# Causal attention and a hardswish feed-forward: the products of weights and v of two pairs of heads in one stretch of TensorE

## The chip, the cores and the metric

The kernel runs on one core of one Trainium2 chip. The metric is the device time of one launch in microseconds (us); lower is better. A core has five engines with a queue each, which meet only at semaphores: PE (TensorE, matrix products, with PEld for its weight loads), DVE (VectorE), ACT (ScalarE), POOL (GpSimd) and SP (SyncE, which issues this kernel's transfers).

## The reference

q, k and v are 4 batches x 12 heads x 448 positions x 64, in float32.

```python
scores = scale * np.matmul(q, k.transpose(0, 1, 3, 2))
scores = np.where(np.triu(np.ones((seq, seq), dtype=bool), k=1), -1000000000.0, scores)
scores = scores - np.max(scores, axis=-1, keepdims=True)
attn = np.exp(scores)
attn = attn / (np.sum(attn, axis=-1, keepdims=True) + 1e-09)
x = np.matmul(attn, v)        # then heads side by side: 1792 rows of 768
h = x @ w_in                  # 768 -> 2048
g = h * np.clip(h + 3.0, 0.0, 6.0) / 6.0
out = g @ w_out               # 2048 -> 768
```

## The kernel before

**Tiling.** The 448 positions of a batch are four tiles of 112. Heads are worked on in pairs, six pairs to a batch. The first 112 positions of all four batches are done first, for each pair (`first_pair`). The other 336 positions of one pair of one batch are the work of `pair(n)`, n = 6 x batch + p, which is called 24 times: scores for three tiles (lines 450 and 451, in batch 0 line 453), masking and row minimum on DVE (L476), exponentials with row sums on ACT (L483), the inverse (L492, L493), the scaling of the weights on POOL (L505), nine transposes on PE in three blocks (L516), a copy of each block out of PSUM into a tile `pt` (through `move`, L238 or L241), and the product with v (`times_v`, L535). That product has eight matmuls: four tiles of positions times two heads. One head's result goes to partitions 0 to 63 of the PSUM bank `av`, the other's to 64 to 127. Its operands are float32, and the trace shows each of them as two matmuls, 16 for a pair.

**Splitting.** `x_split` then takes the bank and makes two float32r tiles of it, `xh` (rounded) and `xl` (the rest). Its steps are a rounding copy on ACT or DVE, for batches 0 and 1 also a plain copy to `r` on ACT, and a subtraction on POOL or DVE. The feed-forward part runs in five groups (`group(g)`): group 0 has 448 columns (first tiles of all batches), groups 1 to 4 the 336 remaining ones of one batch each. Every product is done three times (lines 598 to 600: high x high, high x low, low x high). A chunk of weights is loaded, in group 0 decoded on DVE (L571 to L576, in a PSUM bank `s`), and split into `wh` (ACT) and `wl` (DVE or POOL). A group is 576 matmuls; I call them G below. Group g takes x of batch g-1, and its first G comes 576 G after that of the group before. While a group runs, the attention of a later batch is slipped in between its chunks.

**What sets the order.** All work is recorded as operations with a key (a due time in steps), a duration, the engines that may take it, and the buffers it needs. `Flow.run` plays this forward with its own durations and gives each engine a fixed list: an engine takes the ready operation with the lowest key for which all buffers are free. Buffers are counted by kind: `pt0`, `pt1`, `pt2` 4 each (a pair needs two of each), `vr` 3, `xh` and `xl` 8, `r` 4, and the PSUM banks `s` 6 and `mo` 2. A `pair` has key t = 16 n - 16 (in batch 0: 13 n + 4), and its `times_v` key t + 15.9. `times_v` is recorded as `tiled`, for which the planner adds 0.1 us when PE goes from an untiled operation to a tiled one or back.

Of the kernel before, what the change touches and what calls it, by code (L numbers as in the profile page):

```python
# [43 lines left out]
R = S - C  # L44
# [146 lines left out]
def tile_causal_attention_hardswish_moe(ctx: ExitStack, tc: tile.TileContext, q, k, v, w_in, w_out, out):  # L191
# [13 lines left out]
    def buf(tag, shape, dt=F32):  # L205
        return Buf(tag, shape, dt)

    def bank(tag):
        return Buf(tag, [128, 512], F32)

    def ap(b):
        if b.tile is None:
            b.tile = pools[b.tag].tile(b.shape, b.dt, tag=b.tag, name=b.tag)
        return b.tile

    def f(x):
        return x.bitcast(F32)


    def one(key, ways, dur, emit, r, w):  # L220

        ways = {e: x if isinstance(x, tuple) else (x, 0) for e, x in ways.items()}
        flow.op(key, ways, [(dur, emit, w)], r)

    def pe(key, parts, r, tiled=False):
        flow.op(key, {"PE": (1, 0)}, [(d, lambda e, g=g: g(), w) for d, g, w in parts], r, tiled)
# [7 lines left out]
    def move(key, n, o, i, r, w, ways=None, scale=None):  # L234

        def emit(e):
            if e == "A":
                nc.scalar.copy(o(), i()) if scale is None else nc.scalar.mul(o(), i(), scale)  # L238
            elif e == "D":
                if scale is None:  # L240
                    nc.vector.tensor_copy(o(), i())  # L241
                else:
                    nc.vector.tensor_scalar(o(), i(), scale, None, ALU.mult)
            else:
                nc.gpsimd.tensor_scalar(o(), i(), 1.0, 1.0, ALU.mult, ALU.mult)  # L245
        one(key, ways or {"A": 1}, (n + 200) / 1200, emit, r, w)

    def minus(key, n, o, a, b, r, w, ways):
        def emit(e):
            (nc.gpsimd if e == "P" else nc.vector).tensor_tensor(o(), a(), b(), ALU.subtract)  # L250
        one(key, ways, elem(n), emit, r, w)
# [25 lines left out]
    def x_split(key, g, p, av, n):  # L277
        xh, xl = buf("xh", [128, S], F32R), buf("xl", [128, S], F32R)
        x_t[g, p] = xh, xl
        move(key, n, lambda: ap(xh)[:, :n], lambda: ap(av)[:, :n], [(av, 0)], [(xh, 0)], {"A": 1, "D": (1, .5)})  # L280
        y = av
        if g < 2:
            y = buf("r", [128, S])
            move(key, n, lambda: ap(y)[:, :n], lambda: ap(av)[:, :n], [(av, 0)], [(y, 0)], {"A": 1})
        minus(
            key + .01, n, lambda: ap(xl)[:, :n], lambda: ap(y)[:, :n], lambda: f(ap(xh)[:, :n]),
            [(y, 0), (xh, 0)], [(xl, 0)], {"P": 2.4, "D": (1, 1.0)} if g < 2 else {"D": 1},
        )
# [117 lines left out]


    TILES = (3, 2, 1)

    def pair(n):  # L410
        b, p = divmod(n, NPAIR)
        t = T_REST + 16 * n if b else T_EARLY + 13 * n
        vr = buf("vr", [C, NC_, 2, D])
# [12 lines left out]
        if b:  # L426
            for e in range(2):
                x, y, z = qk[e], op[e], kl[e]
# [12 lines left out]
        st = buf("prow", [C, 2, 8])  # L441
        ps = {(e, i): bank("s") for i in TILES for e in range(2)}
        pr = {(e, i): buf(f"pr{i}", [C, C * (i + 1)]) for i in TILES for e in range(2)}

# [49 lines left out]

        sums = [(st, e, 4 + i) for e in range(2) for i in TILES]
        one(t + 4, {"D": 1}, .45, inverse, [], sums)
        pt = {}
        for e in range(2):
            for i in reversed(TILES):
                def scaled(g, e=e, i=i):  # L500
                    x, r = ap(pr[e, i]), ap(st)[:, e, 4 + i:5 + i]
                    if g == "A":
                        nc.scalar.mul(x, x, r)
                    else:
                        nc.gpsimd.tensor_scalar(x, x, r, 1.0, ALU.mult, ALU.mult)  # L505
# [23 lines left out]
        av = bank("s")  # L529
# [7 lines left out]
                        start=(j == 0), stop=(j == NC_ - 1),  # L537
                    )

        pe(t + 15.9, [(1.9, times_v, [(av, 0)])], [(vr, 0)] + [(x[0], 0) for x in pt.values()], True)  # L540
        x_split(t + 16, b + 1, p, av, R)


    def cols(i):
# [119 lines left out]
    for g in range(B + 1):  # L664
        if g:
            for p in range(NPAIR):
                pair(NPAIR * (g - 1) + p)
        group(g)
# [41 lines left out]
```

## Time and profile before

| | |
|---|---|
| median of 3 runs | 661.43 us (659.28 to 661.99) |
| profiled execution | 661.54 us, of it span 659.8 us |
| PE busy | 643.9 us, 98% |
| DVE, ACT, POOL busy | 465.8, 367.3, 301.2 us |
| mean TensorE clock granted | 0.992 |

The span is the time between the first and the last instruction; the profiled execution took 1.74 us more than it. A row of the timeline gives start, length, engine, line, operation and tiles. The lengths of PE's matmuls overlap, so what one costs is read from start to start. In the change's file the lines from 409 on are numbered one higher, and those behind `times_v` six higher (L535 is L536 there, L598 to L600 are L604 to L606).

### The profile page before, as it was taken

What the parts mean: (1) busy time and instruction counts of PE and PEld (TensorE: products, weight loads), DVE (VectorE), ACT (ScalarE), POOL (GpSimd) and SP (SyncE); (2) the same over time, 40 slices, a digit from 0 to 9 for tenths busy, and PEclk for the clock granted to TensorE, in tenths of its full rate; (3) what the DMA queues carried; (4) which work ended last, traced back from release to release, by engine and by line L of the source; (5) the groups of instructions that cost most, each with busy time, mean ns of one, the idle gap of its engine ahead of it and who ended that gap; (6) DMA issues with size and microseconds to landing.
All of it is one profiled execution on the core that took longest, in us unless ns stands there. A gap on an engine that the chain in (4) does not pass through costs nothing.

```text
span 659.8 us, 12245 instructions
## 1 busy us (share of the span) xinstructions
PE 643.9 (98%) x4236; PEld 587.3 (89%) x4236; DVE 465.8 (71%) x939; ACT 367.3 (56%) x870; POOL 301.2 (46%) x333
## 2 busy tenths in 40 slices
PE   7689999999999999999999999999999999999998
PEld 5569887878889999999999999999999999999997
DVE  4889898977687798854588795567798743566432
ACT  3665656654546666555576664656666554444342
POOL 1667667546572686423375563433676410011100
PEclk9979999999999999999999999999999999999999
DMA  9989876888788543556744547555553334643452
GB/s 232 259 267 298 265 242 192 260 282 295 206 265 246 158 144 107 159 171 182 217 152 135 154 127 206 157 168 186 161 168 87 112 113 132 209 139 110 139 164 65
DMA packets 66878, 120.89 MB, mean 183 GB/s; under 512 B 16896, under 2 KB 33408, under 8 KB 66816
## 3 DMA queue, kind: packets, MB, share of 16 engines
q1 hardware_dynamic: 66816, 120.11, 60.7%
q8 instruction: 33, 0.54, 0.3%
q14 instruction: 29, 0.24, 0.1%
HBM read 101.99 MB, written 18.09 MB: 182 GB/s over the span
## 4 chain that ended last, share of the span: by engine, by line
PE 92%; DVE 3%; DMA 1%; SPq 1%; ACT 1%; POOL 1%; issue 1%; DVEq 0%; ACTq 0%; POOLq 0%
PE mo L598 24%; PE mo L600 23%; PE mo L599 23%; PE s L535 6%; PE s L516 6%; PE s L450 3%; PE s L451 2%; PE s L453 2%; DMA gh<-in_k_dram 1%; SPq L229 1%; PE s L399 1%; DVE s L571 1%; DVE s L573 1%; DVE op L576 0%; PE s L329 0%
## 5 line engine op out<-in xcount | busy, mean ns | idle before, releaser
L250 DVE TENSOR_TENSOR wl<-wd,wh 128x512 fp32r<-128x512 f32 (+1 forms) x159 | 142.8, 898 | 99.8 <-ACT wh L238 99.5
L238 ACT CAST wh<-wd 128x512 fp32r<-128x512 f32 (+1 forms) x160 | 112.9, 706 | 120.0 <-PE mo L599 85.9
L598 PE MATMUL mo<-xh,wh 128*128 128x336 f32 (+1 forms) x480 | 160.8, 335 | 0.1
L598 PE MATMUL mo<-gh,wh 128*128 128x336 f32 (+1 forms) x480 | 159.2, 332 | 0.0
L600 PE MATMUL mo<-xh,wl 128*128 128x336 f32 (+1 forms) x480 | 157.2, 327 | 0.0
L600 PE MATMUL mo<-gh,wl 128*128 128x336 f32 (+1 forms) x480 | 156.9, 327 | 0.3 <-POOL wl L250 0.3
L599 PE MATMUL mo<-gl,wh 128*128 128x336 f32 (+1 forms) x480 | 156.4, 326 | 0.0
L599 PE MATMUL mo<-xl,wh 128*128 128x336 f32 (+1 forms) x480 | 156.2, 325 | 0.0
L505 POOL TENSOR_SCALAR pr<-pr,prow 112x224 f32<-112x224 f32 x144 | 109.0, 773 | 39.5 <-DVE prow L493 39.3
L476 DVE CUSTOM_DVE_ANT_0 s<-s,mask 112x448 f32<-112x448 f32 (+1 forms) x144 | 70.6, 527 | 39.7 <-PE s L451 33.1
L245 POOL TENSOR_SCALAR gh<-r 128x336 fp32r<-128x336 f32 x51 | 33.3, 654 | 138.2 <-DVE r L627 128.6
L598 PEld LDWEIGHTS mo<-xh,wh 128*128 128x128 f32 x480 | 91.0, 190 | 5.8 <-issue 1.7
L598 PEld LDWEIGHTS mo<-gh,wh 128*128 128x128 f32 x480 | 90.3, 188 | 2.8 <-issue 0.8
L599 PEld LDWEIGHTS mo<-xl,wh 128*128 128x128 f32 x480 | 91.4, 190 | 1.1
L600 PEld LDWEIGHTS mo<-gh,wl 128*128 128x128 f32 x480 | 90.2, 188 | 2.2 <-POOL wl L250 0.6
L600 PEld LDWEIGHTS mo<-xh,wl 128*128 128x128 f32 x480 | 90.6, 189 | 1.3
L599 PEld LDWEIGHTS mo<-gl,wh 128*128 128x128 f32 x480 | 90.3, 188 | 1.3
L483 ACT ACTIVATE pr<-s,prow 112x448 f32<-112x448 f32 (+1 forms) x144 | 76.9, 542 | 25.7 <-DVE prow L476 25.7
L250 POOL TENSOR_TENSOR wl<-op,wh 128x512 fp32r<-128x512 f32 (+1 forms) x35 | 53.3, 1522 | 44.1 <-ACT wh L238 34.3
L238 ACT COPY pt<-s 112x336 f32<-112x336 f32 x139 | 53.3, 446 | 26.0 <-PE s L516 25.9
L621 ACT ACTIVATE r<-mo,three 128x336 f32<-128x336 f32 (+1 forms) x80 | 44.7, 558 | 26.4 <-PE mo L600 20.9
L245 POOL TENSOR_SCALAR op<-qk 128x784 fp32r<-128x784 f32 x31 | 30.4, 985 | 57.3 <-PE s L451 54.0
(70 smaller groups left out, 853.6 us busy)
## 6 DMA issues: line engine op xcount, KB each, us to landing
wd<-kept_w SPq DMA_DIRECT2D x64, 384.0 KB, 3.3
wd<-kept_w SPq DMA_DIRECT2D x96, 256.0 KB, 2.7
wd<-in_w_in_dram SPq DMA_DIRECT2D x16, 768.0 KB, 5.7
wd<-in_w_out_dram SPq DMA_DIRECT2D x24, 512.0 KB, 5.2
qk<-in_k_dram SPq DMA_DIRECT2D x84, 112.0 KB, 2.7
qk<-in_q_dram SPq DMA_DIRECT2D x84, 84.0 KB, 2.6
kept_w<-op SPq DMA_DIRECT2D x16, 384.0 KB, 5.7
kept_w<-op SPq DMA_DIRECT2D x24, 256.0 KB, 5.4
```

The lines of the kernel that those rows point to most:

```text
L238: nc.scalar.copy(o(), i()) if scale is None else nc.scalar.mul(o(), i(), scale)
L245: nc.gpsimd.tensor_scalar(o(), i(), 1.0, 1.0, ALU.mult, ALU.mult)
L250: (nc.gpsimd if e == "P" else nc.vector).tensor_tensor(o(), a(), b(), ALU.subtract)
L476: lambda _, e=e, i=i, w=w, dst=dst: nc.vector.tensor_tensor_reduce(dst(), dst(), mask[:, S - w:], -0.125, 3.0e38, ALU.add, ALU.min, ap(st) ...
L483: lambda _, e=e, i=i, dst=dst: nc.scalar.activation(ap(pr[e, i]), dst(), ACTF.Exp, bias=ap(st)[:, e, i:i + 1], scale=-1.0, accum_out=ap(st ...
L505: nc.gpsimd.tensor_scalar(x, x, r, 1.0, ALU.mult, ALU.mult)
L516: nc.tensor.transpose(ap(tp)[:C, C * o:C * o + C], ap(pr[e, i])[:, C * j:C * j + C], ident)
L535: nc.tensor.matmul(ap(av)[64 * e:64 * e + 64, R - w:R], ap(vr)[:, j, e, :], ap(ph)[:, o:o + w], start=(j == 0), stop=(j == NC_ - 1),)
L598: nc.tensor.matmul(ps, ap(wh)[:, a], xh, start=start, stop=False)
L599: nc.tensor.matmul(ps, ap(wh)[:, a], xl, start=False, stop=False)
L600: nc.tensor.matmul(ps, ap(wl)[:, a], xh, start=False, stop=stop)
L621: lambda _, r=r, acc=acc: nc.scalar.activation(ap(r)[:, :n], ap(acc)[:, :n], ACTF.Relu, bias=three, scale=1.0),
```

## The change

The function `pair` no longer records its `times_v` and `x_split` at once. It puts them into a list `left`; every second pair (p odd) records one operation with two parts, the products of the pair before and its own, with the key of the second, and then both splits with that key.

```diff
     TILES = (3, 2, 1)
+    left = []
...
-        pe(t + 15.9, [(1.9, times_v, [(av, 0)])], [(vr, 0)] + [(x[0], 0) for x in pt.values()], True)
-        x_split(t + 16, b + 1, p, av, R)
+
+        left.append((p, av, times_v, [(vr, 0)] + [(x[0], 0) for x in pt.values()]))
+        if p % 2:
+            pe(t + 15.9, [(1.9, go, [(a, 0)]) for _, a, go, _ in left], [x for a in left for x in a[3]], True)
+            for u, a, _, _ in left:
+                x_split(t + 16, b + 1, u, a, R)
+            left.clear()
```

An operation needs all its buffers at its start: two banks `s`, and all twelve `pt`-tiles (four of each kind, two of each for either pair) stay taken until then.

On PE, in batch 1, this stood for its sixth pair before (s_3872 is the bank `av`, vr_3102 that pair's v):

```order
L599 MATMUL mo_3859<-gl_2624,wh_3788 128x336
L600 MATMUL mo_3859<-gh_2608,wl_3793 128x336
L535 MATMUL s_3872<-pt0_3804,vr_3102 64x336
L535 MATMUL s_3872<-pt0_3841,vr_3102 64x336
L535 MATMUL s_3872<-pt1_3818,vr_3102 64x336
L535 MATMUL s_3872<-pt1_3855,vr_3102 64x336
L535 MATMUL s_3872<-pt2_3821,vr_3102 64x224
L535 MATMUL s_3872<-pt2_3857,vr_3102 64x224
L535 MATMUL s_3872<-pt2_3821,vr_3102 64x112
L535 MATMUL s_3872<-pt2_3857,vr_3102 64x112
L450 MATMUL s_3886<-op_3694 112x448
L451 MATMUL s_3886<-kl_3711,op_3694 112x448
```

After the same G of the program the change has a stretch of sixteen. This is its seam, from the last two products of one pair (bank s_3857) on:

```order
L536 MATMUL s_3857<-pt2_3553,vr_2786 64x112
L536 MATMUL s_3857<-pt2_3589,vr_2786 64x112
L536 MATMUL s_3869<-pt0_3789,vr_3346 64x336
L536 MATMUL s_3869<-pt0_3826,vr_3346 64x336
L536 MATMUL s_3869<-pt1_3803,vr_3346 64x336
L536 MATMUL s_3869<-pt1_3840,vr_3346 64x336
L536 MATMUL s_3869<-pt2_3806,vr_3346 64x224
L536 MATMUL s_3869<-pt2_3842,vr_3346 64x224
L536 MATMUL s_3869<-pt2_3806,vr_3346 64x112
L536 MATMUL s_3869<-pt2_3842,vr_3346 64x112
L451 MATMUL s_3884<-op_3678 112x448
L452 MATMUL s_3884<-kl_3696,op_3678 112x448
```

One pair's products follow the other's with nothing between them. The place 96 G earlier, where the pair before had its own stretch, now goes from a G to a score product.

Over the whole of PE's list (from group 0's first G on) such stretches stand at 24 places before and at 12 now. Of transposes it has 52 runs before and 59 now, of scores (L450, L451, L453) 52 both times. The new runs come mostly in group 0. There the first pair of batch 1 had its nine transposes in one run:

```order
L600 MATMUL mo_2336<-gh_694,wl_2324 128x448
L516 MATMUL s_2365<-ident_121,pr1_2237 112x112
L516 MATMUL s_2365<-ident_121,pr2_2221 112x112
L516 MATMUL s_2365<-ident_121,pr3_2201 112x112
L516 MATMUL s_2370<-ident_121,pr1_2237 112x112
L516 MATMUL s_2370<-ident_121,pr2_2221 112x112
L516 MATMUL s_2370<-ident_121,pr3_2201 112x112
L516 MATMUL s_2376<-ident_121,pr2_2221 112x112
L516 MATMUL s_2376<-ident_121,pr3_2201 112x112 x2
L598 MATMUL mo_2336<-gh_694,wh_2357 128x448
```

Now they come block by block, with six G after each:

```order
L606 MATMUL mo_2253<-gh_694,wl_2301 128x448
L517 MATMUL s_2334<-ident_121,pr1_2146 112x112
L517 MATMUL s_2334<-ident_121,pr2_2131 112x112
L517 MATMUL s_2334<-ident_121,pr3_2092 112x112
L604 MATMUL mo_2253<-gh_694,wh_2287 128x448
L605 MATMUL mo_2253<-gl_706,wh_2287 128x448
L606 MATMUL mo_2253<-gh_694,wl_2301 128x448
L604 MATMUL mo_2253<-gh_694,wh_2287 128x448
L605 MATMUL mo_2253<-gl_706,wh_2287 128x448
L606 MATMUL mo_2253<-gh_694,wl_2301 128x448
L517 MATMUL s_2353<-ident_121,pr1_2146 112x112
```

On ACT, behind the last products of batch 0, the split of one pair stood between two castings of weights before:

```order
L238 CAST wh<-op 128x512
L238 CAST xh<-s 128x336
L238 COPY r<-s 128x336
L238 CAST wh<-op 128x512 x2
L483 ACTIVATE pr_2289,prow<-s,prow 112x224
```

Now two pairs are split there at a time; one of the two castings to `xh` is on DVE's list:

```order
L238 CAST wh<-op 128x512 x2
L484 ACTIVATE pr_2209,prow<-s,prow 112x224
L238 COPY r<-s 128x336
L238 CAST xh<-s 128x336
L238 COPY r<-s 128x336
L238 CAST wh<-op 128x512
```

## Rows read from the trace of the kernel before

**Rows 1.** The page: the chain that ended last, share of the span by engine.
```profile
PE 92%; DVE 3%; DMA 1%; SPq 1%; ACT 1%; POOL 1%; issue 1%; DVEq 0%; ACTq 0%; POOLq 0%
```

**Rows 2.** Windows: stretch, its length, busy us of each engine, clock, DMA.
```profile
62.70:162.00 99.30, 98.88 (x561) 81.37 (x561) 86.59 (x180) 56.60 (x134) 63.87 (x65) 1.00 0.81 255
162.00:206.00 44.00, 43.75 (x254) 36.90 (x255) 34.05 (x69) 23.11 (x57) 24.21 (x27) 1.00 0.78 241
206.00:552.70 346.70, 346.70 (x2413) 325.71 (x2411) 247.51 (x507) 211.30 (x508) 171.41 (x191) 1.00 0.52 154
```

**Rows 3.** Timeline of PE at the last pair: start us, length us, engine, line, operation.
```profile
550.60 0.32 PE L600 MATMUL mo<-gh,wl 128*128 128x336 f32 x1
550.85 1.92 PE L535 MATMUL s<-pt,vr 112*64 112x336 f32 x16
552.70 0.42 PE L598 MATMUL mo<-gh,wh 128*128 128x336 f32 x1
552.96 0.32 PE L599 MATMUL mo<-gl,wh 128*128 128x336 f32 x1
553.11 0.32 PE L600 MATMUL mo<-gh,wl 128*128 128x336 f32 x1
```

**Rows 4.** Timeline inside that stretch, by narrow windows: steps two, five and six.
```profile
551.18 0.73 PE L535 MATMUL s<-pt,vr 112*64 112x336 f32 x4
...
552.03 0.55 PE L535 MATMUL s<-pt,vr 112*64 112x224 f32 x4
...
552.22 0.46 PE L535 MATMUL s<-pt,vr 112*64 112x224 f32 x4
```

**Rows 5.** Timeline of PE: a stretch with scores behind it; scores alone.
```profile
206.19 0.32 PE L600 MATMUL mo<-xh,wl 128*128 128x336 f32 x1
...
207.94 0.32 PE L599 MATMUL mo<-xl,wh 128*128 128x336 f32 x1
...
285.88 0.32 PE L600 MATMUL mo<-gh,wl 128*128 128x336 f32 x1
...
289.66 0.32 PE L599 MATMUL mo<-gl,wh 128*128 128x336 f32 x1
```

**Rows 6.** Timeline of PE: scores of batch 0 alone, and with a stretch behind.
```profile
98.80 0.37 PE L600 MATMUL mo<-xh,wl 128*128 128x448 f32 x1
...
99.97 0.37 PE L599 MATMUL mo<-xl,wh 128*128 128x448 f32 x1
...
142.28 0.37 PE L600 MATMUL mo<-gh,wl 128*128 128x448 f32 x1
...
145.30 0.36 PE L599 MATMUL mo<-gl,wh 128*128 128x448 f32 x1
```

**Rows 7.** Timeline of PE around nine transposes, and around three.
```profile
89.25 0.36 PE L600 MATMUL mo<-xh,wl 128*128 128x448 f32 x1
...
90.54 0.36 PE L599 MATMUL mo<-xl,wh 128*128 128x448 f32 x1
90.74 0.36 PE L600 MATMUL mo<-xh,wl 128*128 128x448 f32 x1
...
94.25 0.36 PE L600 MATMUL mo<-xh,wl 128*128 128x448 f32 x1
...
94.96 0.36 PE L599 MATMUL mo<-xl,wh 128*128 128x448 f32 x1
```

**Rows 8.** The line of `times_v`: weight loads, ns least/median/most, first and last start.
```profile
L535 PEld LDWEIGHTS s<-pt,vr x384: 132/137/137, 75.5 to 552.4; 112*64 112x64 f32 x192
```

**Rows 9.** Timeline of PE at 184 us, with the idle time before a matmul.
```profile
184.18 0.37 PE L599 MATMUL mo<-gl,wh 128*128 128x448 f32 x1
184.80 0.47 PE L600 MATMUL mo<-gh,wl 128*128 128x448 f32 x1 [0.25 <-POOL wl L250]
```

**Rows 10.** Timeline of ACT in a split at 184 us.
```profile
183.99 0.44 ACT L238 CAST xh<-s 128x336 fp32r<-128x336 f32 x1 [0.60 <-PE s L535]
```

**Rows 11.** Timeline of PE: group 4's first product with x.
```profile
567.53 0.31 PE L598 MATMUL mo<-xh,wh 128*128 128x336 f32 x1
```

## The prediction

> **What bounds the kernel now.** I read the chain of waits first: PE holds 92% of it, and no other engine more than 3% [rows 1]. Then the busy times by stretch: from 62.7 us, where the first stage ends, to 552.7 us, where the last product with v ends, PE is busy for 98.88 of 99.30, 43.75 of 44.00 and all of 346.70 us [rows 2]. It is without work for 0.7 us in 490. DVE, the next, is at 87% in the first of these stretches and at 71% in the last. So in the part that the change touches a microsecond less on PE is one less in the span, and one that another engine gains gives nothing. What counts is what PE pays that is no column of a product. The clock is at its full level in all three stretches (granted 1.00, so 2.4 GHz), and PE doesn't rest in them, before or after; I take no term for it.
>
> **What one stretch of products with v costs.** Lengths overlap, so I read starts. Between G of 336 columns a step is 0.15 us (552.96 to 553.11). At the last pair [rows 3] the last G before starts at 550.60 and the second G behind at 552.96: 2.36 us, where two steps would be 0.31. The visit costs 2.05 us. Its own work is eight steps, one for each matmul of the program. The 336-column ones are 0.283 us apart (551.18 to 552.03 is three of them), a 224-column one 0.19 [rows 4]; 112 columns I put at half of that, 0.095. That makes 4 x 0.283 + 2 x 0.19 + 2 x 0.095 = 1.70 us. The remaining 0.35 us is the way in and out: the first product starts 0.25 after the last G instead of 0.15, the first step inside takes 0.33 (550.85 to 551.18) instead of 0.28, the last product needs 0.19 (two steps of 0.095 would end at 552.60, and G starts at 552.70), and the first G behind takes 0.26.
>
> With score products behind it, the visit from 285.88 to 289.66 is 3.78 us, and the same scores alone, 206.19 to 207.94, are 1.75 [rows 5]. The difference is 2.03: 1.70 of work and 0.33. With batch 0's scores ahead of it (themselves a product on half of the rows) it is 3.02 against 1.17 us [rows 6], a difference of 1.85, so only 0.15: leaving those scores costs much the same, and is saved.
>
> In PE's list before, eight of the 24 stretches stand between G, thirteen have scores of batches 1 to 3 on one or both sides, and three stand behind scores of batch 0. That is 8 x 0.35 + 13 x 0.33 + 3 x 0.15 = 7.5 us of ways in and out.
>
> **The change part by part.**
>
> Merging. PE's list now has 12 stretches of double length: three between G, eight beside scores, one behind scores of batch 0. 3 x 0.35 + 8 x 0.33 + 0.15 = 3.8 us, 3.7 less than before. The products themselves stay, 384 matmuls in the trace. That a seam between two pairs costs nothing is not in this trace, since no two pairs stand side by side. Its nearest row is a step inside a stretch, where other weights and other columns come in and the step is still 0.283 [rows 4]: no cost. The far bound is that a seam costs what a way in does, 0.10 + 0.05 us, for 12 seams 1.8 us. I take nothing, as the inner step is the same matter: same shape, same halves of the array.
>
> Transposes. Their runs go from 52 to 59, mostly in group 0, where single blocks of three now stand between G. Nine together, 89.25 to 90.54, are 1.29 us less two steps of 0.20, so 0.89; three, 94.25 to 94.96, are 0.71 less 0.40, so 0.31 [rows 7]. Three times three is 0.93, so two more visits cost 0.04. Seven cost 7 x 0.02 = 0.15 us. Score runs are as many as before; some now meet a G where they met a product with v. A visit of eight scores alone costs 1.75 - 0.31 = 1.44 us [rows 5], and its steps (four of about 0.20, four of 0.155) 1.43, so this is under 0.02 for each of some ten places. I put 0.1 to it, and 0.05 to a run of batch 0's scores that had transposes directly behind it and now has a G.
>
> Splits. Two banks come to be split at once. On ACT a casting to `xh` takes 0.44 us [rows 10], the copy to `r` as much, so a merged stretch brings up to 0.9 us more in one go to ACT in batches 0 and 1. That lies beside PE as long as `wh` and `wl` are ready ahead. Where that cover is gone PE waits for the part that sticks out; the trace has one such place, 184.80 us, where a G waits 0.25 us for `wl` from POOL [rows 9]. In groups 1 to 3 PE is never without work. I take no stall more than before, and between -0.3 (the one there goes) and 3 us for the range.
>
> Waiting for the second pair. The first pair of a couple has its products up to a pair's period later. Its x is wanted only in the next group. The tightest is the last couple, which ends where it ends now, at 552.70, and group 4 wants x at 567.53 [rows 11]: 14.8 us for splits of some 2 us. What is held longer are the `pt`-tiles, one `vr`, and `av` not at all, since both banks are taken only at the start. Transposes of the next pair must then wait for free tiles and banks, which in the list has PE do G in between; nothing is queued behind them. Weight and q, k loads on SP's queue keep their distance of chunks, though `vr` loads come later in it; they have a pair's period to arrive.
>
> **Sum.** -3.7 + 0.15 + 0.1 + 0.05 = -3.4 us. The profiled execution took 661.54 us (span 659.8 and 1.74 around it), 0.1 over the median of the three runs shown. 661.5 - 3.4 = 658.1, from the median 658.0. I say 658.1 us, 0.5% less than before.
>
> The Trainium skill speaks for a price of the seams. In "TensorE: Matmul & The Clock Gate", section "Measured speedup vs the span model" with "The mechanism" before it, a weight load runs beside matmuls in flight only when its row group is another. All products with v use the same 112 rows. By that rule each seam would show a load, 0.137 us in this trace [rows 8], 12 x 0.137 = 1.6 us, and the sum would be -1.8. The trace doesn't bear it out inside a stretch: the step of 0.283 has room for no load of its own, though each step has two matmuls with a load each.
>
> **The rivals.**
>
> *A seam costs a way in.* The first product of the second pair has waits of its own (for its v and for ACT's copies), and the 0.15 us of a way in could come from such waits and not from the change of halves. Against it: a run of transposes begins with a wait for POOL's scaling too, and yet a run more costs 0.02 us [rows 7]. Then 1.8 us of the gain go: 659.9 us, within 0.5%.
>
> *The splits stick out.* Group 0 has the thin cover: all of PE's 0.7 us without work lie in its two stretches [rows 2], and one piece of it was a wait for `wl` [rows 9]. If ACT's 0.9 us more came through in full at the three couples of batch 0, 2.7 us would go: 660.8 us. For it speaks that DVE is at 87% there, against it that ACT is at 57% (56.60 of 99.30). The Trainium skill, in "TensorEngine Tiling (Array Packing)", section "PSUM Bottleneck", says that tiling speeds up the products and not the emptying of PSUM, which may then be the limit; by that the price would be this rival's, and no row here has PE wait for a bank yet.
>
> *Slower: banks in the second half of group 0.* Decoding a chunk needs a bank `s`, and between 162 and 206 us six banks serve decoding, the scores and transposes of batch 1's first pairs, and now two results at once. The transposes that come block by block show that tiles or banks are short there. If decoding comes late, `wl` does, and a G waits as at 184.18, where a step of 0.20 took 0.62, 0.42 lost [rows 9]. If all 24 chunks of that half lost as much, 10 us would go: 668.2 us. It decides from 16 chunks on (16 x 0.42 = 6.7 us, the gain and 0.5%). Against it: before, one chunk did.
>
> **How the numbers follow.** A measurement of this kernel can tell about 0.5% from no change, 3.3 us: faster means under 658.1, slower over 664.7. The forecast lies on the first bound. Forecast (the full gain, stalls under 1 us, 657.2 to 659.0): 0.68, of which 0.37 falls under the bound, about half, as it should with the sum on it. Seam: 0.09. Splits sticking out: 0.15. Slower: 0.05. A gain over 4 us, by a stall that goes: 0.03. So faster 0.37 + 0.03 = 0.40, same 0.31 + 0.09 + 0.15 = 0.55, slower 0.05. The range is 656.9 to 660.6: below, the forecast's end and some of the runs' own spread; above, the seam's 659.9 and nearly all of the splits' 660.8.
>
> **What would show it.** In the profile after: 12 stretches of 32 matmuls; between the 16th and 17th start of one a step of 0.09 to 0.10 us, not 0.19 or more; a visit between G of 3.75 us (2 x 1.70 + 0.35) beside the 2.05 of now; PE without idle time from 62.7 us on, and the end of the last stretch at about 549 us. Wrong would be: longer seams, idle time of PE in front of L606 put down to `wl`, or before L517 to POOL or to a copy, above all between 160 and 206 us.

## The result, and the profile after

The change made the kernel slower: 666.44 us median of six runs (665.96 to 668.86) against 660.94 (659.28 to 661.99), a ratio of 1.0092 with a 95% interval of 1.0071 to 1.0113. I had forecast 658.1 us and given "slower" one chance in twenty. The profiled execution, 668.86 us with a span of 667.1, is the longest of the six. 1.6 us of what sets it apart lie ahead of the 79th G, where PE's list is still before's (PE waits 3.3 us behind the 36th; e7 and e8, with before's list, have such a wait there too), so below I compare stretches behind that.

The chain of waits first, where PE had 92% [rows 1]:

```profile
PE 78%; DVE 7%; DMA 5%; POOL 4%; issue 3%; SPq 1%; ACT 1%; DVEq 0%; POOLq 0%; ACTq 0%
```

Then the busy times by stretch (length, busy us of PE, PEld, DVE, ACT, POOL, clock, DMA share, GB/s), the last one up to the end of the last product with v:

```profile
62.70:162.00 99.30, 98.24 (x556) 81.15 (x557) 86.55 (x177) 57.87 (x137) 60.55 (x62) 1.00 0.81 250
162.00:206.00 44.00, 43.54 (x252) 37.12 (x249) 34.29 (x67) 21.81 (x55) 27.33 (x30) 1.00 0.74 231
206.00:559.69 353.69, 349.20 (x2428) 327.39 (x2426) 251.02 (x514) 210.16 (x507) 174.35 (x193) 1.00 0.53 155
```

PE was without work for 0.7 us in these three before [rows 2] and is for 6.0 now, 4.5 of it behind 206 us, where it never waited. The waits of PE behind 62 us (who for whom, us in total, times, longest):

```profile
PE mo L604 <- DVE r L633: 2.1, 3, 1.7
PE s L517 <- POOL pr L506: 1.4, 3, 0.5
PE s L451 <- ACT wh L238: 1.0, 2, 0.5
PE s L517 <- DVE op L582: 0.7, 1, 0.7
PE mo L606 <- POOL wl L250: 0.4, 1, 0.4
PE s L517 <- ACT pt L238: 0.2, 1, 0.2
```

Six kinds of wait, 5.8 us in all, stand where there were two of 0.7 us together; four of them are new. Idle time understates a wait, as it leaves out the overlap with the matmul ahead that the wait takes away: the wait of 1.66 us shown further down delays its G by some 1.8 us from start to start. What I had worked out of the merging itself is there, though. The last couple, in the timeline of PE:

```profile
555.90 0.32 PE L606 MATMUL mo<-gh,wl 128*128 128x336 f32 x1
556.14 3.62 PE L536 MATMUL s<-pt,vr 112*64 112x336 f32 x32
559.69 0.42 PE L604 MATMUL mo<-gh,wh 128*128 128x336 f32 x1
559.95 0.32 PE L605 MATMUL mo<-gl,wh 128*128 128x336 f32 x1
```

From 555.90 to 559.95 are 4.05 us, less two steps of 0.15: a visit of 3.75, as forecast, where two visits cost 4.10 [rows 3]. The seam inside it, by narrow windows (step five of the first pair and of the second):

```profile
557.32 0.55 PE L536 MATMUL s<-pt,vr 112*64 112x224 f32 x4
...
559.02 0.64 PE L536 MATMUL s<-pt,vr 112*64 112x224 f32 x6
```

They are 1.70 us apart, one pair's own work [rows 3, 4], and so it is at all twelve seams: the seam costs nothing. So the gain of some 3.4 us is real, and about 9 us are lost beside it.

To see where, I count G and take, in each trace, the time from the start of the 79th G to that of the last of group 1, and from there to the last of group 3. The differences to the kernel before (262.0 and 241.6 us) add up to the differences of the medians within some 1.2 us in every run below:

| kernel | groups 0 and 1, us | groups 2 and 3, us | median, us | before beside it, us |
|---|---|---|---|---|
| the change | +2.8 | +2.6 | 666.44 | 660.94 |
| e1, moved by hand | -0.8 | -0.8 | 659.58 | 660.62 |
| e2, batches 1 to 3 merged | +1.4 | +2.6 | 664.98 | 660.62 |
| e3, batch 0 merged | +3.3 | 0.0 | 663.64 | 660.62 |
| e4, planner may not put wl on POOL | +1.1 | -0.9 | 660.16 | 660.62 |
| e5, the change, wl on DVE by hand | +2.3 | -0.9 | 662.59 | 660.70 |
| e6, before, 12 wl on POOL by hand | 0.0 | +4.3 | 663.80 | 660.70 |
| e7, e1 with scalings on ACT | -1.5 | -2.3 | 657.06 | 660.70 |
| e8, before with scalings on ACT | 0.0 | -0.3 | 661.12 | 660.70 |
| e9, e5 as two operations | +1.0 | -1.1 | 660.33 | 660.84 |
| e10, e5 with scalings on ACT | +1.1 | -1.3 | 661.64 | 660.84 |

### The profile page after: what moved, and what is told of

The parts are those of the page before. It is cut to its first block, busy times and chain, and to the rows that moved or that the text cites. A ratio compares the mean times of both kernels' runs of the same rounds, so it can differ in the third digit from the quotient of the medians.

```text
span 667.1 us, 12233 instructions
## 1 busy us (share of the span) xinstructions
PE 643.0 (96%) x4236; PEld 586.6 (88%) x4236; DVE 467.7 (70%) x941; ACT 365.3 (55%) x868; POOL 302.4 (45%) x333
## 4 chain that ended last, share of the span: by engine, by line
PE 78%; DVE 7%; DMA 5%; POOL 4%; issue 3%; SPq 1%; ACT 1%; DVEq 0%; POOLq 0%; ACTq 0%
PE mo L604 21%; PE mo L606 20%; PE mo L605 20%; PE s L536 6%; PE s L517 5%; DMA kept_w<-op 3%; POOL pr L506 3%; PE s L451 2%; PE s L452 2%; PE s L454 2%; DMA gh<-in_k_dram 1%; SPq L229 1%; DVE s L579 1%; DVE op L582 1%; DVE s L477 1%
## 5 line engine op out<-in xcount | busy, mean ns | idle before, releaser
L250 DVE TENSOR_TENSOR wl<-wd,wh 128x512 fp32r<-128x512 f32 (+1 forms) x148 | 127.9, 864 | 106.1 <-ACT wh L238 102.1
L606 PE MATMUL mo<-gh,wl 128*128 128x336 f32 (+1 forms) x480 | 156.7, 327 | 0.4 <-POOL wl L250 0.4
L606 PE MATMUL mo<-xh,wl 128*128 128x336 f32 (+1 forms) x480 | 156.8, 327 | 0.0
L606 PEld LDWEIGHTS mo<-xh,wl 128*128 128x128 f32 x480 | 90.8, 189 | 1.6 <-DVE wl L250 0.3
L606 PEld LDWEIGHTS mo<-gh,wl 128*128 128x128 f32 x480 | 90.2, 188 | 2.3 <-POOL wl L250 0.8
L245 POOL TENSOR_SCALAR gh<-r 128x336 fp32r<-128x336 f32 x49 | 28.1, 574 | 133.0 <-DVE r L633 128.6
L245 POOL TENSOR_SCALAR op<-qk 128x784 fp32r<-128x784 f32 x33 | 33.0, 1002 | 57.8 <-PE s L452 36.3
```

What stands on the lines that cost most here:

```text
L606: nc.tensor.matmul(ps, ap(wl)[:, a], xh, start=False, stop=stop)
```

## The experiments

**Merging alone, or the order around it? (e1)** The change lets the planner make a new order of everything. e1 takes before's plan and moves only the first pair's product and split, afterwards (the diff is cut; e1 also has five buffers `vr` instead of three):

```diff
...
+        at = {id(a[4]): a[0] for a in out}
+        to = {id(x): at[id(y)] - 1e-6 for x, y in self.couples}   # first pair's op -> second pair's
+        out = [(to.get(id(o), t), n, e, emit) for t, n, e, emit, o in out]
         out.sort(key=lambda a: a[:2])
...
```

> The planner makes the order of the kernel before; then the first pair's products with v and its split are put directly in front of the second pair's, on each engine, and nothing else is moved (five vr buffers, so that loads need not wait). Theory A, the loss of the change comes from the new order that the planner makes of everything else: this kernel shows the whole gain, 12 visits of about 0.3 us, and no new stalls: 657 to 658 us, 0.5% faster than before, PE without idle time from 206 us on. Theory B, the loss comes from holding the first pair back and splitting two pairs at once, in whatever order: it is slower than before, 663 to 667 us, with PE idle in front of transposes or behind the double stretches.

659.58 us, ratio 0.9982 (0.9965 to 0.9998). Theory B falls: holding back and splitting two at a time do not make the kernel slower. Theory A has the direction and not the size: 1.0 us is gained, not 3.5. The trace shows what took the rest. POOL's scaling and PE's transposes of one pair in batch 1, in the timeline of e1 (its line numbers are nine or more higher):

```profile
258.64 2.94 POOL L515 TENSOR_SCALAR pr<-pr,prow 112x224 f32<-112x224 f32 x3
...
260.88 0.36 PE L526 MATMUL s<-ident,pr 112*112 112x112 f32 x2
261.63 0.88 PE L526 MATMUL s<-ident,pr 112*112 112x112 f32 x7 [0.39 <-POOL pr L515]
```

and the same pair before:

```profile
260.99 2.08 POOL L505 TENSOR_SCALAR pr<-pr,prow 112x224 f32<-112x224 f32 x3
...
263.84 0.93 PE L516 MATMUL s<-ident,pr 112*112 112x112 f32 x8
```

Before, POOL was done at 263.07, 0.77 us ahead of the first transpose. In e1 it is done at 261.58, 0.70 us behind, and the third transpose comes 0.65 us behind the second instead of 0.10; so it is in batches 2 and 3 too. The reason is the visit that is gone. It stood among this pair's scores, and PE now gets from the first of them to the pair's first transposes in 13.90 us instead of 15.92, while DVE's masks don't get shorter. Counted from the start of the pair's last scores (250.57 before, 247.59 in e1) these transposes come as before, 13.27 and 13.29 us later, but the inverse comes 5.96 instead of 5.34 us later, and the three scalings take 2.94 instead of 2.08.

**Which batches? (e2, e3)** The condition of the change with `or not b` (e2) or `or b` (e3) behind `p % 2`.

> Only batches 1 to 3 are merged; batch 0 keeps its products pair by pair. In the profile of the change PE loses about 4.4 us in batches 2 and 3 beside a gain of 1.9, and about 4.9 us more up to the end of batch 1. If each part's loss belongs to its own merged pairs: 660.9 + 2.6 for batches 2 and 3 and about as much as nothing to 2 us for batch 1: 663.5 to 665.5 us. If the loss starts in batch 0 and is carried on: near 660 us or below.

> Only batch 0 is merged; batches 1 to 3 keep their products pair by pair. If each part's loss belongs to its own merged pairs, batch 0 costs its gain of 0.7 us back and 2 to 4 us more: 662 to 664.5 us, and from 330 us on PE has no idle time and the distance to the kernel before stays constant. If the loss is carried on from batch 0: 665 us or above.

664.98 us (1.0057, 1.0038 to 1.0076) and 663.64 (1.0031, 1.0014 to 1.0048). In groups 2 and 3 the loss belongs to their own merged batches: with batch 0 alone merged, they are as before; with the others alone, they lose the change's 2.6 us. In groups 0 and 1 the two losses, 3.3 and 1.4 us, don't add up to the change's 2.8.

**POOL's subtractions (e4, e5, e6).** In the change's plan 12 of the `wl` of groups 1 to 4 are on POOL, before 1. What they do is in the change's timeline in group 2:

```profile
340.49 2.60 DVE L250 TENSOR_TENSOR gl<-r,gh 128x336 fp32r<-128x336 f32 x1
340.86 1.86 POOL L250 TENSOR_TENSOR wl<-wd,wh 128x768 fp32r<-128x768 f32 x1
343.01 0.49 DVE L633 SCALAR_TENSOR_TENSOR r<-r,mo 128x336 f32<-128x336 f32 x1
...
343.53 0.51 DVE L250 TENSOR_TENSOR op<-qk,op 64x336 fp32r<-64x336 f32 x1
...
344.18 0.43 PE L451 MATMUL s<-op 128*112 128x448 f32 x1 [0.48 <-ACT wh L238]
```

DVE's subtraction `gl` takes 0.51 us as a rule and 2.60 here: it ends 0.37 us after POOL's has ended. Behind it come the gate L633 and the subtraction that finishes the `op` of a score product, at 344.04; PE starts that product at 344.18. The profile puts the wait down to ACT's `wh`, which ended at 344.05, but the product reads `op` and not `wh`. Of the 12, four hold up a subtraction on DVE in this way, two in each of groups 2 and 3. At the second place of a group (2.08 us instead of 0.51 at 381.14) the gate and the inverse come late, then the scaling on POOL, and then transposes that wait 0.54 us. e4 takes the way over POOL from the planner, e5 keeps the change's plan and moves the 12 to DVE in the finished lists, e6 puts the same 12 chunks on POOL in before's plan:

```diff
-            {"D": 1.15, "P": (2, .5)} if g else ...      # e4
+            {"D": 1.15} if g else ...
+        if g: flow.other[flow.ops[-1].key] = 'D'         # e5; e6: 'P' for the twelve
```

> The changed kernel, but wl of groups 1 to 4 may only be made on DVE (before, POOL made 1 of them; in the change it makes 12 of 1.86 us, and DVE's subtraction beside them takes 2.60 instead of 0.51 us). Theory C, the loss comes from POOL taking wl and holding DVE up: most of the 9 us of new stalls go, 658 to 661 us. Theory A: only the stalls beside those twelve go, some 2 us in batches 2 and 3: 663.5 to 665.5 us, with the waits of transposes for POOL's scaling and of scores for ACT still there.

> The changed kernel in its own order; only the 12 wl of groups 1 to 4 that stand on POOL are done by DVE, at the same place of the plan. Theory C (POOL's long subtractions hold up DVE's, and PE waits behind DVE): the stalls near the twelve go, in groups 2 and 3 nearly all, 1.5 to 2 us a group: 660 to 662 us. Rival, what e4 gained came from the other order that its planner made: this one stays within 1.5 us of the change, 665 to 667 us, and the stalls near 343, 365 and 383 us are still there.

> The kernel before in its own order, nothing merged; only wl of the same 12 chunks is done by POOL. Theory C alone: the long subtractions on POOL hurt in any order, 3 to 5 us slower than before, 663.5 to 666 us, DVE subtractions beside them of 1.2 us and more. If they hurt only where the merged order has left no cover: under 1.5 us slower.

e4: 660.16 us (0.9988, 0.9976 to 1.0), in theory C's range, though its planner made a new order as well. e5: 662.59 (1.0044, 1.0025 to 1.0063). Each taken against the kernel before beside it, this is 3.6 us under the change: a little above theory C's 660 to 662 us, and by the median clear of its rival's 665 to 667. e6: 663.80 (1.0060, 1.0041 to 1.0079), 3.1 us over before. In e5 groups 2 and 3 go from +2.6 to -0.9. The same two subtractions of DVE there:

```profile
335.88 0.50 DVE L252 TENSOR_TENSOR gl<-r,gh 128x336 fp32r<-128x336 f32 x1
...
337.87 0.51 DVE L252 TENSOR_TENSOR op<-qk,op 64x336 fp32r<-64x336 f32 x1
```

The score product behind them starts at 338.94 without a wait. In e6, where nothing is merged, the same lengthening appears:

```profile
370.09 1.86 POOL L252 TENSOR_TENSOR wl<-wd,wh 128x768 fp32r<-128x768 f32 x1
370.15 2.16 DVE L252 TENSOR_TENSOR gl<-r,gh 128x336 fp32r<-128x336 f32 x1 [0.90 <-POOL gh L247]
```

But PE doesn't come to wait behind that one. What it waits for in groups 2 and 3 of e6 is POOL's scaling (1.5 us of idle time in five waits) and the gate (0.9 in two). The subtraction stands ahead of the scaling in POOL's own queue, and the transposes wait:

```profile
339.83 1.87 POOL L252 TENSOR_TENSOR wl<-wd,wh 128x768 fp32r<-128x768 f32 x1
341.69 2.66 POOL L507 TENSOR_SCALAR pr<-pr,prow 112x224 f32<-112x224 f32 x3
...
343.56 0.54 PE L518 MATMUL s<-ident,pr 112*112 112x112 f32 x2
344.40 0.88 PE L518 MATMUL s<-ident,pr 112*112 112x112 f32 x7 [0.31 <-POOL pr L507]
```

Before, these scalings were done at 342.26, ahead of the transposes:

```profile
338.93 3.33 POOL L505 TENSOR_SCALAR pr<-pr,prow 112x224 f32<-112x224 f32 x3
...
342.64 1.03 PE L516 MATMUL s<-ident,pr 112*112 112x112 f32 x9
```

So these subtractions on POOL cost 3 to 4 us in either order, with the merging or without, but in two ways: in the change they lengthen DVE's work, in e6 they mostly make POOL itself late. For the first way the Trainium skill has a cause: by "GPSIMD Engine Reference", section "Specifications", POOL's SBUF interfaces are shared with VectorE, and there is contention with DVE instructions that have two SBUF inputs. DVE's lengthened subtractions have two, and the trace agrees so far: its masks and gates, with one input in PSUM, keep their 0.63 and 0.51 us beside POOL's subtraction at 374.05. The planner knows durations, not that one engine's choice lengthens another's work.

**The wait for the scaling (e7, e8).** One of a pair's six scalings goes to ACT in the finished lists (batches 1 to 3, first head, widest tile):

```diff
+                if b and not e and i == 3:
+                    flow.other[flow.ops[-1].key] = 'A'
```

> As e1 (first pair's products moved by hand), and of each pair of batches 1 to 3 one of the six scalings, that of the first head's widest tile, is done by ACT instead of POOL. In e1 the transposes of one pair a batch waited 0.55 to 0.65 us for POOL's scaling, which they did not before, since the products that were moved away stood between scores and transposes. Theory D, that wait ate the rest of the gain: it goes, 1.5 to 2 us faster than e1, 657 to 658.3 us. Rival, the rest of the gain went elsewhere (double splits, the clock, what the trace does not show): as e1, 659 to 660.5 us.

> The control to e7: the kernel before, nothing merged, with the same scalings on ACT. By theory D the transposes of batches 1 to 3 wait nowhere in it before, so nothing is won: 660 to 661.5 us. Were it as fast as e7, the merging would have had no part in the gain.

e7: 657.06 us (0.9952, 0.9934 to 0.9970). e8: 661.12 (1.0005, 0.9994 to 1.0016). Theory D holds: 2.5 us under e1, and without merging the same edit gives nothing. In e7 the transposes of the pair shown above come after POOL is done at 258.11, and run through:

```profile
255.59 2.52 POOL L515 TENSOR_SCALAR pr<-pr,prow 112x224 f32<-112x224 f32 x3
...
259.19 1.03 PE L528 MATMUL s<-ident,pr 112*112 112x112 f32 x9
```

All that PE waits for between 60 and 570 us in e7 is as little as before:

```profile
PE s L528 <- ACT pt L247: 0.5, 1, 0.5
PE mo L617 <- POOL wl L259: 0.4, 1, 0.4
```

It is the fastest version, faster than both kernels.

**What is left in groups 0 and 1 (e9, e10).** In e5 these two are still 2.3 us longer than before. The longest wait there, in the change's timeline at the start of group 1:

```profile
206.97 0.62 DVE L477 CUSTOM_DVE_ANT_0 s<-s,mask 112x448 f32<-112x448 f32 x1
...
208.03 0.27 PE L452 MATMUL s<-kl,op 128*112 128x224 f32 x1
...
209.40 0.50 DVE L633 SCALAR_TENSOR_TENSOR r<-r,mo 128x336 f32<-128x336 f32 x1
209.96 0.42 PE L604 MATMUL mo<-xh,wh 128*128 128x336 f32 x1 [1.66 <-DVE r L633]
```

The new order has six score tiles come together there; DVE masks five of them, from 206.97 on, before it gets to the gate that frees a bank `mo`, and PE stands for 1.66 us. e9 records the two products as two operations with one key; e10 is e5 with e7's scalings.

```diff
-            pe(t + 15.9, [(1.9, go, [(a, 0)]) for _, a, go, _ in left], [x for a in left for x in a[3]], True)
+            for _, a, go, rd in left:                    # e9
+                pe(t + 15.9, [(1.9, go, [(a, 0)])], rd, True)
```

> As e5 (the change, wl of groups 1 to 4 on DVE by hand), but the products of the two pairs are recorded as two operations with the same key, so that the planner needn't have both banks and all twelve tiles free at one moment. In e5 group 0 and group 1 are still 0.2 and 2.1 us longer than before, while e1, with before's order, has them 0.4 shorter. Theory A1, the joint demand is what spoils the order there: those two stages come down to 139.0 to 139.6 and 122.0 to 122.8 us, 658.5 to 660.5 us in all. Rival A2, holding the first pair's products back to the second's key spoils it, in one operation or two: group 1 stays over 123.5 us, 661 to 663 us.

> e5 with one scaling of each pair of batches 1 to 3 on ACT, as in e7. If the waits for POOL's scaling that are left in e5 (0.24 and 0.52 us in group 1, pieces in groups 2 and 3) are what keeps it from e7, it comes near 657.5 to 659.5 us; if the rest is the wait for DVE's gate at the start of group 1 (1.9 us) and group 0's, it gains 0.5 to 1.5 us on e5 and no more: 661 to 662 us.

e9: 660.33 us (0.9991, 0.9979 to 1.0003), e10: 661.64 (1.0016, 0.9999 to 1.0034). e9's total is in A1's range, but its stages aren't: group 1 is 123.4 us, between the two theories, and group 0 is 139.6, as in e5. The 1.66 us wait is gone, and transposes wait for scaling and copies at other places instead. In e9's list only seven couples stand joined, so that PE makes 17 visits and gives back some of the merging's gain. That doesn't decide between joint demand and holding back. e10 gains 1 us on e5, as the second case had it, though that lies within the two intervals, and keeps the wait for the gate.

## Why the prediction was wrong

**Right, by the traces:** PE bounds; a visit of double length costs 3.75 us; the seam is free (rival one falls, and so does the price by the Trainium skill's rule on weight loads that the prediction took from "TensorE: Matmul & The Clock Gate", section "The mechanism": 1.70 us from step five to step five); the price of a way in and out, of transposes in threes (0.31 us) and of score visits. Where these alone act, in e7, the gain is 3.6 us by the medians; the sum had 3.4, after 0.15 paid for transposes that e7 doesn't split, so 3.6 without that.

**The step that failed** is in "Splits": "I take no stall more than before, and between -0.3 and 3 us for the range". The stalls are 5.5 + 3.4 = 9 us. None of PE's waits is put down to a split, and they don't lie mainly in the half of group 0 in which I put the slower rival. Two of the signs that I had named came, most of them later than I looked for them: PE idle in front of L517 for POOL (1.4 us in three waits) and in front of L606 for `wl` (0.4 us, once). The runs show three parts, sized here by the stages of the table:

- About 4 us: the planner's new order has POOL make 12 of the `wl`, which holds up DVE, and PE behind it (e5: 4.0 us, 3.6 by the medians; in e6 the same 12 cost 3 to 4 us without merging). I had compared PE's list and three pieces of others, and not counted which engine took what; the lists showed 12 against 1.
- About 1.5 us (e10 against e5; by the medians 1.1, which is within their spread): the visit that was taken out from among a pair's scores had been the cover of DVE's masks and POOL's scaling. In before's order this is clear of the spread: e7 is 2.5 us under e1. I asked what the late product holds up, and not what comes early. In the change's own order the transposes behind G 774 and 858 come 0.22 and 0.52 us late by their starts. Those behind 1434 and 2010, 0.70 us late each, belong to the first part: in e5 they run through.
- The rest, some 3.5 us (e10 against e7), 2.6 of it in groups 0 and 1: waits for the gate behind DVE's masks, for decoding on DVE (0.7 us before transposes in the first half of group 0), for copies and scaling. It belongs to the new order, since e1, with the same products merged and before's order, has none of the waits for the gate and for decoding. Which of the planner's constraints makes that order is open: e9 took one away and got 1.3 us back (2.4 by the medians).

"In groups 1 to 3 PE is never without work" was true of a list that the change replaces. I carried the absence of stalls over to an order whose waits I hadn't looked at. And "no row here has PE wait for a bank yet" held for the rows shown alone: the trace before has PE's transposes wait 0.42 us at 117.23 us for ACT's copy out of a bank.

## What to carry to other kernels

When a planner makes the order, a small edit is a new program: compare every engine's share of work in the lists before and after, above all of operations that lengthen another engine's in the trace, and don't carry "no stalls" over from the old order. Work that is taken off the bounding engine was also the cover of what its next instruction waits for; look for the producer whose lead is less than what is removed (here a lead of 0.77 us against a visit of 2.05). If only the merging is wanted, move just that in the finished order, as e1 does, and then relieve the producer that has become late.

## What the runs showed of the hardware

- Switching PE between whole products and two half-width ones and back costs 0.33 to 0.35 us a visit between G or beside the scores of batches 1 to 3, and a second pair of half-width products directly behind costs none of it (1.70 us from step five to step five).
- A subtraction of two SBUF tiles on DVE takes 0.49 to 0.51 us (128x336) where POOL does nothing beside it, and up to 2.60 while POOL subtracts two SBUF tiles for 1.86 us: it ended 0.37 us behind POOL's. DVE's masks and gates, with one input in PSUM, kept their 0.63 and 0.51 us.
- Three scalings on POOL, 2.08 us in one execution, took 2.94 in another at the same place of the program (e1), beside other work of DVE.
